# Windowed attention and a squared-ReLU block in one kernel: larger Q and K load chunks, immediate activation biases, and one deadline key for all engine orders

## The chip, the cores and the metric

The kernel runs on one core of a Trainium2 chip. The metric is the device time of one execution in microseconds (us), as a median of several executions. The profile is that of one execution; its span is about 1.8 us shorter than the time of that run. A run counts as slow when it took over 1.5% longer than the fastest run of the same kernel in its call; ratios are of fast runs alone.

Names of engines in the profile: PE is TensorE (matmuls), PEld its weight loads, DVE is VectorE, ACT is ScalarE, POOL is GpSimd and SPq the queue of SyncE. L467 is a line of the kernel's source.

## The reference

Attention with a window of 32 positions to each side, over 8 batches, 8 heads, 576 positions of 64 values. Its output, 4608 tokens of 512 values, goes through a feed-forward block of width 2048.

```python
scores = q @ k.T / sqrt(64);  mask = |i - j| <= 32        # per batch and head
attn   = softmax(where(mask, scores, -1e9)) @ v
x      = attn.transpose(0, 2, 1, 3).reshape(4608, 512)
h      = x @ w_in                                          # 512 -> 2048
out    = (s * relu(h)**2 + b) @ w_out                      # 2048 -> 512
```

All inputs are float32; the matmuls take bf16.

## The kernel before

The work is a graph of tasks. Each task has an engine, a modelled cost, the data that it reads and writes, and a key. A planner runs the graph once on modelled time, at every step taking the task that can start earliest, and among equals the one with the smallest key. The order so found becomes each engine's fixed instruction order, with the semaphore waits added. So the model of time decides the order, and on the chip an engine whose next instruction waits for a late load holds up everything behind it.

```python
c = (max(free[s], t.ready), t.key, t.n)         # the smallest c is placed next
...
if t.dma is not None:                           # a transfer: one modelled queue for all
    dma_free = max(dma_free, st + 1300.0) + t.dma[1]
    t.fin = dma_free + 700.0
```

One unit of attention is one batch, 192 positions (t = 0, 1, 2) and four heads (g2 = 0, 1): 48 units. Matmuls make the scores (sc), ScalarE the exponential (ex), VectorE multiplies by the mask, matmuls make row sums (ss) and values (av), ScalarE makes the reciprocal by Ln and Exp (rec), and VectorE writes the token columns (xt). The feed-forward block works on token blocks of 384, 128, 256, 384, then 512: for each block 16 groups of 4 matmuls (w), Relu (r), square (gt), then the second matmuls (o).

The q and k of batches 0 and 1 are loaded in three chunks of 192 rows on 96 partitions, cast by VectorE, transposed by TensorE and copied out of PSUM ("evacuated"). Unit 0 needs q chunk 0 and, for its window, k chunks 0 and 1; units 2 and 3 need k chunk 2 as well.

```python
def load2(b, n, t, waits=()):                               # 192 rows on 96 partitions
    ... STG[n][0:96, 2*t:2*t+2, :] ...  src[b, :, 192*t:192*t+192, :]
    key=key_of(b, -16), dma=("l", 768 * 27 / 16.0)

def key_of(b, part): return 16 * (b - 1) + part             # loads -16, casts -8, transposes -6
# attention unit number n: key = -100 + n      feed-forward: key = m + ft / 16

steps = [("q", 0), ("k", 0), ("k", 1), 0, ("q", 1), ("k", 2), 1, ("q", 2), 2]
e.activation(EX[e_][:, :, :], SC[:, :, :], AF.Exp, bias=ZERO_F[:, :], scale=0.125)
```

The softmax here doesn't subtract the row's maximum and nothing guards it: scores larger than these inputs give would overflow.

## Time and profile before

The median was 355.79 us (353.55 to 356.66, 4 runs).

To see where time is lost I count, for each stretch of time, the TensorE work done in it at full rate, from the weight loads in the trace. A w group is counted as its columns times 4 / 2.4 ns and an o matmul as 213 ns (in the trace, unhindered w matmuls of 384 columns start 0.163 us apart and o matmuls 0.215). Eight sc or ss matmuls are counted as 0.34 us, eight av as 0.22 and eight transposes as 0.43 (the trace has 0.33 for sc, 0.57 for ss and av together, and 0.44). This is an estimate. Elapsed time minus work is the "time lost" by TensorE.

| before, stretch of the span (us) | time lost | what the views show there |
|---|---|---|
| 0 to 42 | 30.0 | loads; the first w matmul starts at 35.4; all matmuls up to 40.0 run at half speed |
| 42 to 120 | 13.8 | waits of TensorE, and a spell of half clock |
| 120 to the end | 11.9 | no wait of note; 3.7 us of it after the last matmul |

The busy time of TensorE by stretch, before (stretch, its length, busy us and instructions, granted clock, DMA share, GB/s):

```profile
0.00:36.00 36.00, 14.90 (x187) 1.00 1.09 199
36.00:60.00 24.00, 23.82 (x158) 1.00 1.16 209
60.00:90.00 30.00, 26.64 (x303) 1.00 0.98 185
90.00:120.00 30.00, 24.82 (x227) 0.94 1.04 179
120.00:150.00 30.00, 29.58 (x256) 1.00 1.12 208
```

TensorE idles most before 36 us, then between 60 and 120 us. What it waited for, before (instruction and line, what released it: total us, times, longest):

```profile
PE w L431 <- DVE natq L414: 7.2, 2, 6.2
PE w L431 <- DVE natk L414: 6.8, 2, 5.5
PE ss L480 <- DVE ex L467: 5.6, 5, 2.2
PE o L577 <- DVE outs L589: 2.6, 1, 2.6
```

The first two are the head: transposes waiting for casts, which wait for loads. The last two are waits for VectorE in the middle. The timeline of VectorE in the head, before (start, us, instruction; in brackets the idle time ahead of it and what ended it):

```profile
12.21 1.01 DVE L436 COPY kt<-o 128x768 bf16<-128x768 bf16 x1
18.59 0.69 DVE L414 CAST natk<-stgk 96x1024 bf16<-96x1024 f32 x1 [5.37 <-DMA stgk<-in_k_dram]
19.20 0.42 DVE L390 CAST vb<-stgv 128x512 bf16<-128x512 f32 x1
20.20 1.01 DVE L436 COPY kt<-w 128x768 bf16<-128x768 bf16 x1 [0.58 <-PE w L431]
21.11 0.67 DVE L467 TENSOR_TENSOR ex<-ex,mask 128x1024 bf16<-128x1024 bf16 x1
```

VectorE stood for 5.4 us at the cast of a late k chunk; the mask of unit 0, ready since its exponential ended at 15.0 us, came after it at 21.1. The groups of ScalarE instructions, before (busy us, mean ns of one):

```profile
L464 ACT ACTIVATE ex<-sc,zero 128x1024 bf16<-128x1024 f32 x48 | 53.3, 1110 | 11.5 <-PE sc L457 11.4
L565 ACT ACTIVATE r_27<-w,zero 128x512 bf16<-128x512 f32 x24 | 16.5, 687 | 14.4 <-PE w L559 14.4
```

### The profile page before, as it was taken

The numbers are of one execution on the slowest core, as the hardware profiler recorded it, in microseconds if no ns is written. First come the engines' busy times: TensorE is split into PE (matmuls) and PEld (weight loads), VectorE is DVE, ScalarE is ACT, GpSimd is POOL, SyncE is SP. The second block draws the span as 40 slices with busy tenths as digits, with TensorE's granted clock in tenths as the row PEclk, the third lists the DMA queues.
The fourth block names the chain that finished last, engine by engine and source line by source line (L and its number), as shares of the span: only waits on it lengthen the run. The fifth ranks groups of instructions, "written<-read, shape, count | busy, mean of one in ns | idle before, by whom it ended". The sixth has DMA issues, their size and how long they took to land.

```text
span 353.1 us, 6377 instructions
## 1 busy us (share of the span) xinstructions
PE 316.8 (90%) x2502; PEld 161.2 (46%) x2544; DVE 208.9 (59%) x467; ACT 207.4 (59%) x324; POOL 49.4 (14%) x68
## 2 busy tenths in 40 slices
PE   1256999699976999999999999999999999999995
PEld 1134456465543444444444444444444444445542
DVE  4466368888696657866777767754345345432321
ACT  2249543678765668767777666666466456643310
POOL 8803023101530220130012000000000000000000
PEclk9999999999999899999999999999999999999999
DMA  7999999996998999999899997630000000010102
GB/s 167 211 210 207 221 203 200 207 219 122 189 216 160 196 188 200 210 223 174 187 196 183 173 218 174 127 105 32 30 32 30 32 30 32 30 61 30 59 38 83
DMA packets 107806, 49.45 MB, mean 140 GB/s; under 512 B 87552, under 2 KB 100864, under 8 KB 107776
## 3 DMA queue, kind: packets, MB, share of 16 engines
q1 hardware_dynamic: 100416, 35.40, 51.7%
q0 software_dynamic: 7360, 13.64, 19.9%
q8 instruction: 20, 0.33, 0.4%
q14 instruction: 10, 0.08, 0.1%
HBM read 36.70 MB, written 9.44 MB: 131 GB/s over the span
## 4 chain that ended last, share of the span: by engine, by line
PE 74%; DMA 12%; SPq 5%; DVE 4%; ACT 3%; issue 2%
PE o L577 32%; PE w L559 32%; DMA stgq<-in_q_dram 9%; PE ss L480 4%; SPq L309 4%; PE sc L457 3%; PE av L480 3%; DMA stgk<-in_k_dram 3%; SPq L320 1%; ACT ex L464 1%; DVE ex L467 1%; DVE vb L390 1%; DVE gt L568 1%; ACT rec L487 1%; DVE xt L494 1%
## 5 line engine op out<-in xcount | busy, mean ns | idle before, releaser
L559 PE MATMUL w<-xt,win 128*128 128x512 bf16 (+3 forms) x690 | 149.6, 346 | 2.6 <-ACT r_28 L565 0.9
L577 PE MATMUL o<-wout,gt 128*128 128x512 bf16 x548 | 140.0, 380 | 4.7 <-DVE outs L589 2.6
L559 PEld LDWEIGHTS w<-xt,win 128*128 128x128 bf16 x704 | 64.0, 99 | 66.2 <-issue 3.2
L577 PEld LDWEIGHTS o<-wout,gt 128*128 128x128 bf16 x576 | 53.2, 98 | 60.5 <-DVE outs L589 2.8
L464 ACT ACTIVATE ex<-sc,zero 128x1024 bf16<-128x1024 f32 x48 | 53.3, 1110 | 11.5 <-PE sc L457 11.4
L309 POOL DMA_DIRECT2D stgv<-in_v_dram x48 | 39.8, 833 | 139.6 <-DVE vb L390 104.3
L565 ACT ACTIVATE r_26<-w,zero 128x512 bf16<-128x512 f32 (+3 forms) x44 | 26.8, 608 | 28.9 <-PE w L559 28.2
L467 DVE TENSOR_TENSOR ex<-ex,mask 128x1024 bf16<-128x1024 bf16 x48 | 33.1, 689 | 17.8 <-ACT ex L464 17.1
L565 ACT ACTIVATE r_29<-w,zero 128x512 bf16<-128x512 f32 (+3 forms) x44 | 26.8, 608 | 21.5 <-PE w L559 21.1
L565 ACT ACTIVATE r_27<-w,zero 128x512 bf16<-128x512 f32 (+3 forms) x44 | 26.8, 609 | 21.0 <-PE w L559 20.5
L565 ACT ACTIVATE r_28<-w,zero 128x512 bf16<-128x512 f32 (+3 forms) x44 | 26.8, 608 | 20.2 <-PE w L559 20.2
L487 ACT ACTIVATE rec<-ss,zero 128x384 f32<-128x384 f32 x48 | 27.7, 576 | 17.2 <-PE ss L480 17.1
L589 DVE SCALAR_TENSOR_TENSOR outs<-o,sb_34,cvec 128x512 f32<-128x512 f32 x36 | 26.9, 748 | 13.7 <-PE o L577 13.7
L494 DVE TENSOR_TENSOR xt<-av,rec 128x384 bf16<-128x384 f32 x48 | 26.5, 553 | 8.6 <-ACT rec L490 4.5
L490 ACT ACTIVATE rec<-rec,zero 128x384 f32<-128x384 f32 x48 | 29.4, 612 | 0.7
L568 DVE TENSOR_TENSOR gt<-r_29 128x512 bf16<-128x512 bf16 (+3 forms) x44 | 16.4, 373 | 21.3 <-ACT r_29 L565 21.0
L568 DVE TENSOR_TENSOR gt<-r_28 128x512 bf16<-128x512 bf16 (+3 forms) x44 | 16.4, 373 | 20.3 <-ACT r_28 L565 20.2
L568 DVE TENSOR_TENSOR gt<-r_27 128x512 bf16<-128x512 bf16 (+3 forms) x44 | 16.4, 374 | 19.4 <-ACT r_27 L565 19.1
L480 PE MATMUL ss<-ex,ones 128*64 128x128 bf16 x384 | 21.2, 236 | 7.2 <-DVE ex L467 5.6
L568 DVE TENSOR_TENSOR gt<-r_26 128x512 bf16<-128x512 bf16 (+3 forms) x44 | 16.4, 373 | 13.9 <-ACT r_26 L565 13.8
L480 PEld LDWEIGHTS ss<-ex,ones 128*64 128x64 bf16 x384 | 13.0, 115 | 25.0 <-DVE ex L467 7.5
L390 DVE CAST vb<-stgv 128x512 bf16<-128x512 f32 (+1 forms) x48 | 21.0, 443 | 4.9 <-PE av L480 4.1
(52 smaller groups left out, 154.7 us busy)
## 6 DMA issues: line engine op xcount, KB each, us to landing
out_dram<-outs SPq DMA_DIRECT2D x36, 256.0 KB, 2.4
stgq<-in_q_dram SPq DMA_DIRECT2D x24, 256.0 KB, 5.5
stgk<-in_k_dram SPq DMA_DIRECT2D x24, 256.0 KB, 5.6
stgv<-in_v_dram POOLq DMA_DIRECT2D x16, 256.0 KB, 7.1
stgv<-in_v_dram POOLq DMA_DIRECT2D x16, 192.0 KB, 7.9
stgq<-in_q_dram SPq DMA_DIRECT2D x6, 384.0 KB, 13.4
stgk<-in_k_dram SPq DMA_DIRECT2D x6, 384.0 KB, 12.0
stgv<-in_v_dram POOLq DMA_DIRECT2D x16, 128.0 KB, 5.9
```

What stands on the lines that cost most here:

```text
L309: lambda e: e.dma_start(STG[n][p0:p1, blk, :].rearrange("p (h d) -> p h d", h=H), src_of[n][b, :, s0:s0 + ns, :].rearrange("h s d -> s h d ...
L464: add("act", lambda e: e.activation(EX[e_][:, :, :], SC[:, :, :], AF.Exp, bias=ZERO_F[:, :], scale=0.125), 1130.0, reads=[("SC", 0), ("SC" ...
L467: add("dve", lambda e: e.tensor_tensor(EX[e_][:, :, :], EX[e_][:, :, :], MASK[:, :, :], ALU.mult), 700.0, reads=[("E", e_), "MASK"], write ...
L480: fns.append(lambda e, u=u, a=a, hh=hh, dst=dst, lhs=lhs: e.matmul(dst[64 * hh:64 * hh + 64, 192 * u + 64 * a:192 * u + 64 * a + 128], lhs ...
L487: add("act", lambda e: e.activation(REC[e_][:, :], SS[:, 0:384], AF.Ln, bias=ZERO_F[:, :], scale=1.0), 600.0, reads=["SS", "ZERO"], writes ...
L490: add("act", lambda e: e.activation(REC[e_][:, :], REC[e_][:, :], AF.Exp, bias=ZERO_F[:, :], scale=-1.0), 600.0, reads=[("REC", e_), "ZERO ...
L494: add("dve", lambda e: e.tensor_tensor(XT[:, prs[0]:prs[1] + 1, x0:x0 + 192], AV[:, 0:384].rearrange("p (u c) -> p u c", u=2), REC[e_][:, ...
L559: add("pe", [lambda e, kc=kc: e.matmul(W[wb][:, 0:nt], lhsT=WIN_BF[:, kc, ft * 128:(ft + 1) * 128], rhs=XT[:, kc, t0:t0 + nt], start=(kc = ...
L565: add("act", lambda e: e.activation(R1[rb][:, 0:nt], W[wb][:, 0:nt], AF.Relu, bias=ZERO_F[:, :], scale=1.0), 280 + 0.82 * nt, reads=[("W", ...
L568: add("dve", lambda e: e.tensor_tensor(GT[gs][:, ft, 0:nt], R1[rb][:, 0:nt], R1[rb][:, 0:nt], ALU.mult), 160 + 0.53 * nt, reads=[("R1", rb ...
L577: add("pe", [lambda e, fc=fc: e.matmul(O[ob][:, :], lhsT=GT[gs][:, fc, sub * 128:sub * 128 + 128], rhs=WOUT_BF[:, fc, :], start=(fc == 0), ...
L589: add("dve", lambda e: e.scalar_tensor_tensor(OUTS[us][:, :], O[ob][:, :], SB128[:, 0:1], CVEC[:, :], ALU.mult, ALU.add), 760, reads=[("O" ...
```

## The change

It has three parts. Q and K of batches 0 and 1 come in chunks of 256 rows on 128 partitions (256, 256 and 64 rows), so unit 0 needs one chunk each of q and k; every chunk is evacuated in two halves. Activations take an immediate bias. Every key is on one scale, the feed-forward position at which the result is due, and the planner's transfers are modelled a little later. The diff, cut to its core:

```diff
+    DMALAT = 600.0
-                    r = t.fin + (100.0 if t.dma is not None else t.lat)
+                    r = t.fin + (self.DMALAT if t.dma is not None else t.lat)
...
         def key_of(b, part):
-            return 16 * (b - 1) + part
+            if b == 0:
+                return -100 + part
+            t = min(2, max(0, int(part + 0.5)))
+            return rel[b, t, 0] / 16.0 + 0.1 * (part - t) - (0 if part >= 0 else 0.5)
...
-        def load2(b, n, t, waits=()):                      # 96 partitions, 192 rows
+        CHUNKS = [(256 * c, min(128, (S - 256 * c) // 2)) for c in range((S + 255) // 256)]
+        def load2(b, n, c, waits=()):
+            s0, ns = CHUNKS[c]
...          # transpose_pe: two halves r = 0, 1; batch 0: r = 0 on ScalarE, r = 1 on VectorE
-            add(evac, fn, 900, reads=[res], writes=grans(n, slot, 192 * t, 192 * t + 192), key=key)
+                add(evac, fn, 200 + 4 * ns / 1.0, reads=[res],
+                    writes=grans(n, slot, s0, s0 + 2 * ns), key=key, accum=(r == 1))
...          # keys: first two v blocks of batch 0 -2000; casts, copies and units by key_of
-            key = -100 + n
+            key = key_of(b, t + 0.1 * g2)
...
-                steps = [("q", 0), ("k", 0), ("k", 1), 0, ("q", 1), ("k", 2), 1, ("q", 2), 2]
+                steps = [("q", 0), ("k", 0), 0, ("k", 1), ("q", 1), 1, ("k", 2), ("q", 2), 2]
...
-            ... AF.Exp, bias=ZERO_F[:, :], scale=0.125)    # and Ln, Exp, Relu
+            ... AF.Exp, bias=0.0, scale=0.125)
```

More of the change, by code (lines that the diff above doesn't have):

```diff
@@ L259, in bass_sliding_window_symmetric__then__act_starrelu_kernel @@
         IDENT = sb((128, 128), BF16, "ident")
-        ZERO_F = sb((128, 1), F32, "zero")
         GT = [sb((128, 16, 512), BF16, "gt") for _ in range(2)]
@@ L286, in bass_sliding_window_symmetric__then__act_starrelu_kernel, with first_block @@
         NPE = 2
-        EVAC0 = {"q": "act", "k": "dve"}
+        EVACS = [("act", "dve"), ("dve", "dve")]
+        def first_block(tok):
+            return next(m for m in range(NM) if TBLK[m][0] + TBLK[m][1] > tok)
+        rel, nxt = {}, 1e9
+        for b in range(B - 1, 0, -1):
+            for t in range(NT3 - 1, -1, -1):
+                for g2 in (1, 0):
+                    nxt = min(nxt - PACE, 16 * first_block(b * S + 192 * t) - LEAD)
+                    rel[b, t, g2] = nxt
         src_of = {"q": q, "k": k, "v": v}
@@ L312, in load @@
                 ),
-                900.0 if n == "v" else 1070.0, writes=[("STG", n, blk)], key=key_of(b, -16), waits=waits,
-                dma=("v" if n == "v" else "l", ns * 9.3))
-        def load2(b, n, t, waits=()):
+                900.0 if n == "v" else 1070.0, writes=[("STG", n, blk)], waits=waits,
+                key=-2000 if b == 0 and n == "v" and blk < 2 else key_of(b, -5),
+                dma=("v" if n == "v" else "l", ns * 9.4))
+        CHUNKS = [(256 * c, min(128, (S - 256 * c) // 2)) for c in range((S + 255) // 256)]
+        def load2(b, n, c, waits=()):
+            s0, ns = CHUNKS[c]
             return add(
@@ L320, in load2 @@
                 lambda e: e.dma_start(
-                    STG[n][0:96, 2 * t:2 * t + 2, :].rearrange("p a (h x) -> p (a h) x", h=NPAIR),
-                    src_of[n][b, :, 192 * t:192 * t + 192, :].rearrange("h (p r) d -> p h (r d)", r=2),
-                ),
-                1000.0, writes=[("STG", n, 2 * t), ("STG", n, 2 * t + 1)], key=key_of(b, -16), waits=waits,
-                dma=("l", 768 * 27 / 16.0))
+                    STG[n][0:ns, 2 * c:2 * c + 2, :].rearrange("p a (h x) -> p (a h) x", h=NPAIR),
+                    src_of[n][b, :, s0:s0 + 2 * ns, :].rearrange("h (p r) d -> p h (r d)", r=2),
+                ),
+                1000.0, writes=[("STG", n, 2 * c), ("STG", n, 2 * c + 1)], key=key_of(b, -5), waits=waits,
+                dma=("l", 8 * ns * 26 / 16.0))
         def load_weights(which, i, waits=()):
@@ L335, in load_weights @@
                     moe_w_out.rearrange("(fc p) c -> p fc c", p=128)[:, 4 * i:4 * i + 4, :])
-            return add("pool", fn, 1000.0, writes=[("W" + which, i)], waits=waits, key=-30,
+            return add("pool", fn, 1000.0, writes=[("W" + which, i)], waits=waits, key=key_of(0, 0),
                        dma=("w", 2550.0))
-        for n, t in (("q", 0), ("k", 0), ("k", 1), ("q", 1), ("k", 2), ("q", 2)):
-            load2(0, n, t)
+        for n, c in (("q", 0), ("k", 0), ("k", 1), ("q", 1), ("k", 2), ("q", 2)):
+            load2(0, n, c)
         for blk in range(6):
             load(0, "v", blk)
-        add("dve", lambda e: e.memset(ZERO_F[:], 0.0), 100, writes=["ZERO"], key=-99)
-        add("dve", lambda e: e.memset(ONESW[:], 1.0), 150, writes=["ONESW"], key=-99)
-        add("dve", lambda e: e.memset(ONES[:], 1.0), 150, writes=["ONES"], key=-99)
-        add("dve", lambda e: e.memset(ONES[0:WIN, 1, :], 0.0), 100, writes=["ONES"], key=-98)
-        add("dve", lambda e: e.memset(ONES[128 - WIN:128, 2, :], 0.0), 100, writes=["ONES"], key=-98)
+        add("dve", lambda e: e.memset(ONESW[:], 1.0), 150, writes=["ONESW"], key=-2001)
+        add("dve", lambda e: e.memset(ONES[:], 1.0), 150, writes=["ONES"], key=-2001)
+        add("dve", lambda e: e.memset(ONES[0:WIN, 1, :], 0.0), 100, writes=["ONES"], key=-2000)
+        add("dve", lambda e: e.memset(ONES[128 - WIN:128, 2, :], 0.0), 100, writes=["ONES"], key=-2000)
         for slot in range(2):
@@ L352, in bass_sliding_window_symmetric__then__act_starrelu_kernel @@
                 add("dve", lambda e, slot=slot, c0=c0: e.memset(KT[slot][:, :, c0:c0 + WIN], 0.0), 150,
-                    writes=[("KTPAD", slot)], key=-98)
+                    writes=[("KTPAD", slot)], key=-2000)
         for (p0, blk) in ((0, 0), (128 - WIN, 2 * NT3 - 1)):
             add("dve", lambda e, p0=p0, blk=blk: e.memset(STG["v"][p0:p0 + WIN, blk, :], 0.0), 350,
-                writes=[("STGPAD", blk)], key=-98)
+                writes=[("STGPAD", blk)], key=-2000)
         add("pool", [lambda e: e.dma_start(SB128[:, 0:1], moe_s.partition_broadcast(128)),
                      lambda e: e.dma_start(SB128[:, 1:2], moe_b.partition_broadcast(128))],
-            2000.0, writes=["SB128"], dma=("w", 200.0), key=-60)
+            2000.0, writes=["SB128"], dma=("w", 200.0), key=key_of(0, 4))
         def band(tile, res, lo, hi):
@@ L366, in band @@
                                           channel_multiplier=-1),
-                350, reads=["ONESW"], writes=[res], key=-70)
+                350, reads=["ONESW"], writes=[res], key=-1900)
             add("pool",
@@ L371, in band @@
                                           channel_multiplier=1),
-                350, reads=[res], writes=[res], key=-70)
+                350, reads=[res], writes=[res], key=-1900)
         band(IDENT[:, :], "IDENT", 0, 0)
@@ L377, in bass_sliding_window_symmetric__then__act_starrelu_kernel @@
         add("dve", lambda e: e.tensor_copy(MASK[:, 0, 256:512], MASK[:, 0, 0:256]), 200,
-            reads=["MASK"], writes=["MASK"], key=-40)
+            reads=["MASK"], writes=["MASK"], key=key_of(0, -0.3))
         add("dve", lambda e: e.tensor_copy(MASK[:, 1, :], MASK[:, 0, :]), 250,
-            reads=["MASK"], writes=["MASK"], key=-40)
+            reads=["MASK"], writes=["MASK"], key=key_of(0, -0.3))
         wts = [load_weights("in" if i < 4 else "out", i % 4) for i in range(8)]
@@ L386, in cast_v @@
             slot = b % 2
-            key = key_of(b, -8)
+            key = key_of(b, blk // 2 - 0.3)
             pad = [("STGPAD", blk)] if blk in (0, 2 * NT3 - 1) else []
@@ L402, in cast @@
             add("dve", lambda e: e.tensor_copy(NAT[n][0:ns, blk, :], STG[n][0:ns, blk, :]),
-                400.0, reads=[("STG", n, blk)], writes=[("NAT", n, blk)], key=key_of(b, -8))
+                400.0, reads=[("STG", n, blk)], writes=[("NAT", n, blk)], key=key_of(b, max(0, 128 * blk - WIN) // 192 - 0.5))
         def transpose_dma(b, n, blk):
@@ L410, in transpose_dma, with cast2 @@
                 1250.0, reads=[("NAT", n, blk)], writes=grans(n, slot, s0, s0 + ns),
-                dma=("t", 1000.0), key=key_of(b, -6))
-        def cast2(b, n, t):
+                dma=("t", 1000.0), key=key_of(b, max(0, 128 * blk - WIN) // 192 - 0.4))
+        def cast2(b, n, c):
+            ns = CHUNKS[c][1]
             add("dve", lambda e: e.tensor_copy(
-                NAT[n][0:96, 2 * t:2 * t + 2, :].rearrange("p r (h d) -> p r h d", h=H),
-                STG[n][0:96, 2 * t:2 * t + 2, :].rearrange("p a (g r d) -> p r (a g) d", r=2, d=D)),
-                700.0, reads=[("STG", n, 2 * t), ("STG", n, 2 * t + 1)],
-                writes=[("NAT", n, 2 * t), ("NAT", n, 2 * t + 1)], key=key_of(b, -8))
+                NAT[n][0:ns, 2 * c:2 * c + 2, :].rearrange("p r (h d) -> p r h d", h=H),
+                STG[n][0:ns, 2 * c:2 * c + 2, :].rearrange("p a (g r d) -> p r (a g) d", r=2, d=D)),
+                700.0, reads=[("STG", n, 2 * c), ("STG", n, 2 * c + 1)],
+                writes=[("NAT", n, 2 * c), ("NAT", n, 2 * c + 1)], key=key_of(b, c - 0.5))
@@ L420, in bass_sliding_window_symmetric__then__act_starrelu_kernel, with transpose_pe @@
         tcount = {"n": 0}
-        def transpose_pe(b, n, t, banks, evac):
+        def transpose_pe(b, n, c, banks, evacs):
             slot = b % 2
+            s0, ns = CHUNKS[c]
             dst = QT[slot] if n == "q" else KT[slot]
-            res, bank = banks[tcount["n"] % len(banks)]
-            tcount["n"] += 1
-            view = bank.bitcast(BF16)[:, 0:768].rearrange("p (r g c) -> p r g c", r=2, g=NPAIR)
-            c0 = 192 * t + (0 if n == "q" else WIN)
-            to = dst[:, :, c0:c0 + 192].rearrange("p g (x r) -> p r g x", r=2)
-            key = key_of(b, -6)
-            add("pe", [lambda e, r=r, pr=pr: e.transpose(view[:, r, pr, :],
-                                                         NAT[n][0:96, 2 * t + r, pr * 128:(pr + 1) * 128],
-                                                         IDENT[0:96, 0:96])
-                       for r in range(2) for pr in range(NPAIR)],
-                450, reads=[("NAT", n, 2 * t), ("NAT", n, 2 * t + 1), "IDENT"], writes=[res], key=key)
-            fn = (lambda e: e.copy(to, view)) if evac == "act" else (lambda e: e.tensor_copy(to, view))
-            add(evac, fn, 900, reads=[res], writes=grans(n, slot, 192 * t, 192 * t + 192), key=key)
@@ new lines, in transpose_pe @@
+            c0 = s0 + (0 if n == "q" else WIN)
+            key = key_of(b, c - 0.4)
+            for r in range(2):
+                res, bank = banks[tcount["n"] % len(banks)]
+                tcount["n"] += 1
+                view = bank.bitcast(BF16)[:, 0:512].rearrange("p (g c) -> p g c", g=NPAIR)[:, :, 0:ns]
+                to = dst[:, :, c0:c0 + 2 * ns].rearrange("p g (x r) -> p r g x", r=2)[:, r]
+                add("pe", [lambda e, pr=pr, r=r, view=view: e.transpose(
+                    view[:, pr, :], NAT[n][0:ns, 2 * c + r, pr * 128:(pr + 1) * 128], IDENT[0:ns, 0:ns])
+                    for pr in range(NPAIR)],
+                    270, reads=[("NAT", n, 2 * c), ("NAT", n, 2 * c + 1), "IDENT"], writes=[res], key=key)
+                evac = evacs[r]
+                fn = ((lambda e, to=to, view=view: e.copy(to, view)) if evac == "act" else
+                      (lambda e, to=to, view=view: e.tensor_copy(to, view)))
+                add(evac, fn, 200 + 4 * ns / 1.0, reads=[res],
+                    writes=grans(n, slot, s0, s0 + 2 * ns), key=key, accum=(r == 1))
@@ L461, in unit @@
                             start=True, stop=True))
-            add("pe", fns, 310.0, reads=qk_res, writes=[("SC", 0), ("SC", 1)], key=key + (0.5 if b > 0 else 0),
+            add("pe", fns, 310.0, reads=qk_res, writes=[("SC", 0), ("SC", 1)], key=key + (0.05 if b > 0 else 0),
                 after=after + ([("av", n - 1)] if b > 0 else []), name=("qk", n))
             add("act", lambda e: e.activation(EX[e_][:, :, :], SC[:, :, :], AF.Exp,
-                                              bias=ZERO_F[:, :], scale=0.125),
-                1130.0, reads=[("SC", 0), ("SC", 1), "ZERO"], writes=[("E", e_)], key=key)
+                                              bias=0.0, scale=0.125),
+                1040.0, reads=[("SC", 0), ("SC", 1)], writes=[("E", e_)], key=key)
             add("dve", lambda e: e.tensor_tensor(EX[e_][:, :, :], EX[e_][:, :, :], MASK[:, :, :],
@@ L487, in unit @@
             add("act", lambda e: e.activation(REC[e_][:, :], SS[:, 0:384], AF.Ln,
-                                              bias=ZERO_F[:, :], scale=1.0),
-                600.0, reads=["SS", "ZERO"], writes=[("REC", e_)], key=key)
+                                              bias=0.0, scale=1.0),
+                500.0, reads=["SS"], writes=[("REC", e_)], key=key)
             add("act", lambda e: e.activation(REC[e_][:, :], REC[e_][:, :], AF.Exp,
-                                              bias=ZERO_F[:, :], scale=-1.0),
-                600.0, reads=[("REC", e_), "ZERO"], writes=[("REC", e_)], key=key)
+                                              bias=0.0, scale=-1.0),
+                500.0, reads=[("REC", e_)], writes=[("REC", e_)], key=key)
             x0 = b * S + q0
@@ L498, in unit @@
                 560.0, reads=["AV", ("REC", e_)], writes=[("XT", b, t, g2)], key=key)
-        def first_block(tok):
-            return next(m for m in range(NM) if TBLK[m][0] + TBLK[m][1] > tok)
-        rel, nxt = {}, 1e9
-        for b in range(B - 1, 0, -1):
-            for t in range(NT3 - 1, -1, -1):
-                for g2 in (1, 0):
-                    nxt = min(nxt - PACE, 16 * first_block(b * S + 192 * t) - LEAD)
-                    rel[b, t, g2] = nxt
         for b in range(B):
@@ L535, in bass_sliding_window_symmetric__then__act_starrelu_kernel @@
                     cast2(b, *x)
-                    transpose_pe(b, *x, banks, EVAC0[x[0]] if b == 0 else "dve")
+                    transpose_pe(b, *x, banks, EVACS[b])
                     continue
@@ L565, in s1 @@
             add("act", lambda e: e.activation(R1[rb][:, 0:nt], W[wb][:, 0:nt], AF.Relu,
-                                              bias=ZERO_F[:, :], scale=1.0),
-                280 + 0.82 * nt, reads=[("W", wb), "ZERO"], writes=[("R1", rb)], key=key)
+                                              bias=0.0, scale=1.0),
+                190 + 0.82 * nt, reads=[("W", wb)], writes=[("R1", rb)], key=key)
             add("dve", lambda e: e.tensor_tensor(GT[gs][:, ft, 0:nt], R1[rb][:, 0:nt], R1[rb][:, 0:nt],
```

## The prediction

> **What bounds the kernel now.** Three parts, from the timeline and the busy time by stretch.
> (1) Head, 0 to 35.4 us: the first w<-xt,win matmul starts at 35.4, after only some 13 us of TensorE work. Loads bound it: the DMA share is above 1.1 from 8 us on. The traced packets show how: the SyncE queue (q, k; 512-byte packets, about 45 ns) has moved 1.8 MB by 12 us but needs until 24 us for the last 0.5 MB, because the GpSimd queue (v, weights; about 3 KB and 230 ns a packet) takes the engines. The Trainium skill ("DMA: Bandwidth & Descriptors", on arbitration) says an engine alternates between queues packet by packet; this agrees. Engine order adds to it: the exp of unit 0 ends at 15.0 us, its mask multiply starts at 21.1, since VectorE, in order, first sits 5.4 us on the third k chunk (landed at 18.6).
> (2) 35.4 to 120 us: about 69 us of matmul work (estimate from matmul counts at 2.4 columns/ns) takes 84.6. The TensorE waits show 2.6 us at 64.6 (VectorE held by batch 1's last q chunk), 1.8 at 99.5, 0.9 at 111, 2.2 at 114 (VectorE holding casts of late loads): planning errors rather than bandwidth, the DMA share being 0.95 at 80 to 120. A half-clock spell near 115 us costs 1.7.
> (3) After 120 us TensorE never waits: 230 us, and 3.7 of tail.
>
> **What the change does.**
> - 256-row chunks: unit 0 needs one q and one k chunk (1.05 MB) instead of three of 0.39 MB. The first two v blocks move ahead, so k lands no earlier than about 9 us. The middle units need the first 512 rows of q and k (2.1 MB), on the traced curve there at 18 to 20 us. The last q/k landing of batch 0 stays near 24 us: same bytes.
> - Evacuation: 6 copies of 1.01 us become 12 smaller ones split between ScalarE and VectorE: about -0.3 us latency per chunk.
> - Immediate bias: the Trainium skill ("ScalarE: Activation LUTs", What ACT_TABLE_LOAD costs) gives 280 ns + 0.833 N with a pointer, 186 + 0.833 N without. The trace has 1110 ns for N=1024, 687 for 512; I expect 1020 and 595. Some 320 x 93 ns = 30 us of ScalarE (59% busy), hidden after 120 us; in the head 0.25 us per unit, and block 0's 16 W groups, paced by two banks and ScalarE, gain about 0.7. In all 1 us.
> - New keys and later landings in the plan: the 6 us VectorE block in the head should go; attention of batches 1 to 3 should be placed where its data has come, saving 3 to 5 us of waits between 60 and 120.
>
> **Sum.** First w matmul at about 30 us (-5.5), ScalarE -1, middle waits -4: 355.8 - 10 = about 346.
>
> **Right or wrong.** Right: mask multiply of unit 0 before 15 us; first w matmul at 28 to 32; TensorE waits after it under 4 us; ex activation 1.02 us; part (3) still about 230 us. Wrong if: VectorE again waits on a late chunk ahead of ready work; weights issued sooner starve the second q and k chunks beyond 22 us; or TensorE, now earlier, waits near 60 us for batch 1.
>
> Predicted 346.0 us, 8 in 10 between 339.5 and 352.5; faster by over 2%: 0.67, within 2%: 0.29, slower: 0.04.

## The result, and the profile after

The kernel after took 345.86 us in the median (345.07 to 346.57, 4 runs). The ratio is 0.973, with a 95% interval of 0.968 to 0.978. (A ratio is the mean time of one kernel's fast runs over that of the other's of the same rounds, so it is not quite the ratio of the medians.)

TensorE by stretch, after:

```profile
0.00:36.00 36.00, 18.02 (x206) 1.00 1.11 211
36.00:60.00 24.00, 23.79 (x182) 1.00 1.14 220
60.00:90.00 30.00, 29.16 (x310) 1.00 0.95 199
90.00:120.00 30.00, 25.93 (x247) 1.00 1.11 190
120.00:150.00 30.00, 29.58 (x243) 1.00 1.12 202
```

Busy time in the stretch from 60 to 90 us rose from 26.6 to 29.2 us. In time lost (elapsed minus work at full rate; the repeat is the unchanged kernel after in a later call):

| stretch (us) | before | after | gain | repeat |
|---|---|---|---|---|
| 0 to 42 | 30.0 | 25.7 | 4.3 | 25.1 |
| 42 to 60 | 0.1 | 0.4 | -0.3 | 0.3 |
| 60 to 90 | 5.6 | 2.6 | 3.0 | 2.6 |
| 90 to 120 | 8.1 | 5.6 | 2.5 | 2.4 |
| 120 to the end | 11.9 | 13.0 | -1.1 | 13.2 |

The span fell by 8.3 us (353.1 to 344.8), 4.3 of them in the head, although the first w matmul moved by 5.4 (35.4 to 30.0). Part of what had stood before that matmul, attention of the last two units of batch 0, now stands behind it: the scores of one unit and the row sums and values of two, less one group of values that was behind it before, 1.2 us of work (an estimate from the same counts). A marker that moves by 5.4 us is not a gain of 5.4 us. Nor does the place of the cut leave the gain alone: cut at 36 us, in the middle of the half speed of before, the head would seem to gain only 2.1 us.

What TensorE waited for, after:

```profile
PE w L452 <- DVE natq L433: 9.5, 1, 9.5
PE o L452 <- DVE natq L433: 4.4, 1, 4.4
PE sc L480 <- DMA kt<-natk: 3.4, 1, 3.4
PE ss L503 <- DVE ex L490: 1.5, 5, 0.4
```

Waits for VectorE in the middle are down to 0.4 us each. One wait of 3.4 us is new, for a transposing transfer of k. VectorE in the head, after:

```profile
13.96 0.73 DVE L458 COPY kt<-o 128x512 bf16<-128x512 bf16 x1 [0.67 <-ACT kt L457]
18.97 0.69 DVE L433 CAST natq<-stgq 128x1024 bf16<-128x1024 f32 x1 [4.28 <-DMA stgq<-in_q_dram]
19.58 0.72 DVE L458 COPY kt<-w 128x512 bf16<-128x512 bf16 x1
20.31 0.42 DVE L408 CAST vb<-stgv 64x512 bf16<-64x512 f32 x1
20.77 0.69 DVE L490 TENSOR_TENSOR ex<-ex,mask 128x1024 bf16<-128x1024 bf16 x1
```

The block is still there: the mask of unit 0 starts at 20.8 us, behind 4.3 us of waiting for the second q chunk. The plan thought that chunk would land at 10.8 us.

Score matmuls of units 0 to 3 start at 13.3, 20.1, 22.8 and 25.9 us before, and at 14.7, 20.7, 22.5 and 25.1 after: hardly different. But the columns of unit 3, which the first w matmul needs, are written at 34.5 us before and at 29.9 after. The difference arises after the scores. ScalarE before, in that stretch (cut):

```profile
28.27 1.13 ACT L464 ACTIVATE ex<-sc,zero 128x1024 bf16<-128x1024 f32 x1
30.41 1.11 ACT L464 ACTIVATE ex<-sc,zero 128x1024 bf16<-128x1024 f32 x1 [0.51 <-PE sc L457]
31.42 0.57 ACT L487 ACTIVATE rec<-ss,zero 128x384 f32<-128x384 f32 x1
32.23 1.11 ACT L464 ACTIVATE ex<-sc,zero 128x1024 bf16<-128x1024 f32 x1 [0.24 <-PE sc L457]
33.24 0.60 ACT L490 ACTIVATE rec<-rec,zero 128x384 f32<-128x384 f32 x1
```

And after (cut):

```profile
25.74 1.02 ACT L487 ACTIVATE ex<-sc 128x1024 bf16<-128x1024 f32 x1 [0.59 <-PE sc L480]
28.22 0.49 ACT L510 ACTIVATE rec<-ss 128x384 f32<-128x384 f32 x1 [0.30 <-PE ss L503]
28.74 0.52 ACT L513 ACTIVATE rec<-rec 128x384 f32<-128x384 f32 x1
29.59 1.02 ACT L487 ACTIVATE ex<-sc 128x1024 bf16<-128x1024 f32 x1 [0.33 <-PE sc L480]
```

Some 2.5 of the 4.6 us are there at the start of unit 3's exponential (28.3 us against 25.7): before, ScalarE first did the copy of the third q chunk (26.4 us), the reciprocal of unit 1 and half of that of unit 2. The rest comes next: before, the exponentials of units 4 and 5 (30.4 and 32.2 us) ran ahead of the end of unit 3's reciprocal, 33.8. After, that reciprocal ends at 29.3 and the exponential of unit 4 follows it. The same ScalarE groups after:

```profile
L487 ACT ACTIVATE ex<-sc 128x1024 bf16<-128x1024 f32 x48 | 49.1, 1022 | 10.5 <-PE sc L480 9.6
L578 ACT ACTIVATE r_27<-w 128x512 bf16<-128x512 f32 x24 | 14.3, 597 | 16.5 <-PE w L572 15.2 <-DVE outs L602 1.1
```

An activation is 88 to 90 ns shorter.

### The profile page after: what moved, and what is told of

Its sections match the earlier page's. It is cut to its first block, busy times and chain, and to the rows that moved or that the text cites. A ratio compares the mean times of both kernels' runs of the same rounds, so it can differ in the third digit from the quotient of the medians.

```text
span 344.8 us, 6390 instructions
## 1 busy us (share of the span) xinstructions
PE 314.9 (91%) x2504; PEld 159.8 (46%) x2544; DVE 211.2 (61%) x475; ACT 181.6 (53%) x327; POOL 48.1 (14%) x68
## 4 chain that ended last, share of the span: by engine, by line
PE 83%; DMA 7%; DVE 4%; issue 2%; SPq 1%; ACT 1%; DVEq 0%
PE w L572 36%; PE o L590 35%; DMA stgq<-in_q_dram 4%; PE ss L503 4%; PE sc L480 4%; PE av L503 3%; DMA kt<-natk 3%; PE o L611 1%; DVE vb L408 1%; DVE xt L517 1%; SPq L339 1%; ACT ex L487 1%; PE sc L452 1%; DVE ex L490 1%; DVE natk L420 0%
## 5 line engine op out<-in xcount | busy, mean ns | idle before, releaser
L572 PE MATMUL w<-xt,win 128*128 128x512 bf16 (+3 forms) x689 | 146.3, 342 | 2.3 <-issue 1.1
L572 PEld LDWEIGHTS w<-xt,win 128*128 128x128 bf16 x704 | 62.8, 98 | 61.1 <-DVE xt L517 0.9
L324 POOL DMA_DIRECT2D stgv<-in_v_dram x48 | 38.9, 812 | 140.5 <-DVE vb L408 121.0
L487 ACT ACTIVATE ex<-sc 128x1024 bf16<-128x1024 f32 x48 | 49.1, 1022 | 10.5 <-PE sc L480 9.6
L578 ACT ACTIVATE r_26<-w 128x512 bf16<-128x512 f32 (+3 forms) x44 | 22.9, 520 | 28.2 <-PE w L572 26.2
L578 ACT ACTIVATE r_25<-w 128x512 bf16<-128x512 f32 (+3 forms) x44 | 22.8, 518 | 26.2 <-PE w L572 24.0
L578 ACT ACTIVATE r_27<-w 128x512 bf16<-128x512 f32 (+3 forms) x44 | 22.8, 519 | 23.3 <-PE w L572 22.0
L578 ACT ACTIVATE r_28<-w 128x512 bf16<-128x512 f32 (+3 forms) x44 | 22.8, 519 | 23.1 <-PE w L572 23.0
L510 ACT ACTIVATE rec<-ss 128x384 f32<-128x384 f32 x48 | 23.4, 488 | 21.6 <-PE ss L503 21.5
L602 DVE SCALAR_TENSOR_TENSOR outs<-o,sb_33,cvec 128x512 f32<-128x512 f32 x36 | 26.9, 748 | 12.0 <-PE o L590 11.7
L517 DVE TENSOR_TENSOR xt<-av,rec 128x384 bf16<-128x384 f32 x48 | 26.6, 554 | 10.8 <-PE av L503 8.0
L581 DVE TENSOR_TENSOR gt<-r_26 128x512 bf16<-128x512 bf16 (+3 forms) x44 | 16.4, 374 | 21.5 <-ACT r_26 L578 21.3
L581 DVE TENSOR_TENSOR gt<-r_27 128x512 bf16<-128x512 bf16 (+3 forms) x44 | 16.4, 374 | 20.9 <-ACT r_27 L578 20.9
L581 DVE TENSOR_TENSOR gt<-r_28 128x512 bf16<-128x512 bf16 (+3 forms) x44 | 16.4, 373 | 18.4 <-ACT r_28 L578 18.1
L513 ACT ACTIVATE rec<-rec 128x384 f32<-128x384 f32 x48 | 24.9, 519 | 0.7
L480 PE MATMUL sc<-qt,kt 64*128 64x128 bf16 x384 | 20.3, 229 | 3.7 <-DMA kt<-natk 3.4
L503 PEld LDWEIGHTS ss<-ex,ones 128*64 128x64 bf16 x384 | 12.8, 114 | 20.2 <-issue 5.3
## 6 DMA issues: line engine op xcount, KB each, us to landing
stgk<-in_k_dram SPq DMA_DIRECT2D x4, 512.0 KB, 12.8
```

Of the source, the lines that this page charges most:

```text
L324: lambda e: e.dma_start(STG[n][p0:p1, blk, :].rearrange("p (h d) -> p h d", h=H), src_of[n][b, :, s0:s0 + ns, :].rearrange("h s d -> s h d ...
L480: fns.append(lambda e, u=u, pr=pr, a=a, hh=hh: e.matmul(SC[:, hh, 256 * u + 128 * a:256 * u + 128 * a + 128], lhsT=KT[slot][64 * hh:64 * h ...
L487: add("act", lambda e: e.activation(EX[e_][:, :, :], SC[:, :, :], AF.Exp, bias=0.0, scale=0.125), 1040.0, reads=[("SC", 0), ("SC", 1)], wr ...
L503: fns.append(lambda e, u=u, a=a, hh=hh, dst=dst, lhs=lhs: e.matmul(dst[64 * hh:64 * hh + 64, 192 * u + 64 * a:192 * u + 64 * a + 128], lhs ...
L513: add("act", lambda e: e.activation(REC[e_][:, :], REC[e_][:, :], AF.Exp, bias=0.0, scale=-1.0), 500.0, reads=[("REC", e_)], writes=[("REC ...
L517: add("dve", lambda e: e.tensor_tensor(XT[:, prs[0]:prs[1] + 1, x0:x0 + 192], AV[:, 0:384].rearrange("p (u c) -> p u c", u=2), REC[e_][:, ...
```

## The experiments

Twelve kernels ran, in four calls; all gave right results. The kernel before ran in each call too, with medians of 356.8, 356.5, 357.1 and 355.5 us. The last column is time lost in the profiled run. Every profiled run was fast.

| run | what it is | median us (range) | first w matmul | lost to 42 / 42 to 120 / rest |
|---|---|---|---|---|
| before | | 355.79 (353.55 to 356.66) | 35.4 | 30.0 / 13.8 / 11.9 |
| after | | 345.86 (345.07 to 346.57) | 30.0 | 25.7 / 8.6 / 13.0 |
| a_again | after, unchanged | 344.39 (342.84 to 348.87) | 29.5 | 25.1 / 5.3 / 13.2 |
| b_imm | before, immediate biases | 355.03 (352.66 to 357.37) | 37.0 | 31.0 / 15.3 / 11.8 |
| a_ptr | after, pointer biases | 344.70 (343.70 to 345.49) | 30.3 | 27.4 / 5.6 / 13.1 |
| a_192 | after, old chunks | 349.51 (348.09 to 350.09) | 32.7 | 27.4 / 6.0 / 15.4 |
| a_oldkeys | after, old keys and transfer model | 351.72 (351.11 to 353.30) | 35.1 | 28.7 / 9.4 / 14.4 |
| a_oldmodel | after, old transfer model | 348.20 (344.64 to 348.49) | 28.9 | 25.1 / 9.6 / 14.5 |
| a_late | after, head's true landings, third chunks kept back | 353.81 (352.20 to 355.98) | 28.2 | 27.6 / 10.9 / 17.2 |
| a_late8 | a_late, later loads 8 us later in the plan | 349.30 (346.66 to 352.35) | 28.3 | 25.7 / 12.9 / 12.8 |
| a_holdk | a_late's idea, weights issued later | 350.19 (346.94 to 351.36) | 27.0 | 24.3 / 14.5 / 13.3 |
| a_hold8 | a_holdk, later loads 8 us later in the plan | 348.85 (345.86 to 351.53) | 28.5 | 25.3 / 7.7 / 17.3 |
| a_par | after, halves evacuated without waiting for each other | 348.35 (346.30 to 351.01) | 29.1 | 25.1 / 5.1 / 17.9 |
| a_swap | after, one move in the head | 344.85 (342.70 to 347.84) | 28.5 | 24.3 / 6.5 / 14.3 |

Medians and ranges hold every run. One run each of a_again, a_late8, a_hold8 and a_swap was slow; their fast runs alone have medians of 342.9, 348.0, 348.2 and 344.4. Of a_late's 27.6, 2.6 us are one wait at 39.4 us. The expectation of the repeat, which is the yardstick of its call:

> The kernel after once more, unchanged, as the yardstick of this call: 345 to 346 us, first w matmul at 30 us, and qk of unit 2 at 22.5 us.

Two fast runs of one kernel differ by up to 5 us in the last three calls. The two profiles of the kernel after show one reason: the 3.4 us wait for the transposing transfer is in one and absent from the other. Differences under 2 us between runs of different calls say nothing here.

### The biases

Theory: ScalarE's shorter instructions give about 1 us (the prediction's term). Rival: ScalarE paces the head, so they give 3.

```diff
-  e.activation(EX[e_][:, :, :], SC[:, :, :], AF.Exp, bias=ZERO_F[:, :], scale=0.125)
+  e.activation(EX[e_][:, :, :], SC[:, :, :], AF.Exp, bias=0.0, scale=0.125)     # b_imm; a_ptr is the reverse
```

No engine's order changes in either, apart from the one memset of the bias tile that a_ptr needs.

> The kernel before with immediate biases alone; every engine's order is unchanged. Arithmetic theory (the prediction's ScalarE term): 1 us off, about 354.8 us, first w matmul near 34.5 us. Rival theory (ScalarE paces the head, since it is 6.6 us busy in the 8 us from 24 to 32): 3 us or more off, first w matmul before 33 us.

> The kernel after with the biases as [128,1] pointers again; every engine's order is unchanged. Prediction's ScalarE term: about 1 us slower than the kernel after (347 us), ex activation back to 1.11 us. Rival (ScalarE paces the head): 2.5 us or more slower (348.5 or more).

Measured: b_imm took 355.03 us beside 356.8, but its ratio is 1.001 (0.991 to 1.011), and its first w matmul came at 37.0, not by 34.5. a_ptr took 344.70 us beside 356.8, ratio 0.971 (0.964 to 0.978), the same as the kernel after within error, with its ex back at the old length. So no gain is seen from the 26 us of ScalarE time that the change saves (207.4 to 181.6 us busy), and a_ptr shows no sign of the rival's 2.5 us. The intervals are 2.5 to 3.5 us wide to each side, so the 1 us of the prediction is not excluded.

### The chunks, and the keys

Theory (the prediction): the chunks bring the head's gain. Rival: engine order does, since the scores start at the same times in both kernels.

```diff
 # a_192: load2, cast2, transpose_pe and the step order of before; keys on the new scale by the unit that needs the chunk
-        CHUNKS = [(256 * c, ...)]
+        load2: 192 rows on 96 partitions, one evacuation copy a chunk
 # a_oldkeys: every key, DMALAT and the transfer costs of before; 256-row chunks kept
-            t = min(2, max(0, int(part + 0.5)))
-            return rel[b, t, 0] / 16.0 + ...
+            return 16 * (b - 1) + part
```

> The kernel after with the 192-row chunks, single evacuation copies and step order of before, new keys and immediate biases kept. Prediction (the head's 5.4 us come from the chunks' data arrival): first w matmul back at 34 us or later, 350 us or more. Rival (the head's gain is order and ScalarE time, since the qk matmuls of units 2 and 3 start at 22.8 and 25.9 us before and 22.5 and 25.1 after): first w matmul at 31 us or earlier, at most 347.5 us.

> The kernel after with the keys and the transfer model of before; 256-row chunks and immediate biases kept. Prediction: the head keeps its gain (first w matmul by 31 us), the middle waits come back (about 8 us in all after 36 us), about 350 us. Rival (order makes the head's gain): first w matmul at 33 us or later, 352 us or more.

Measured: without the chunks 349.51 us, first w at 32.7, ratio 0.985 (0.979 to 0.991). Without the keys 351.72 us, first w at 35.1, ratio 0.993 (0.987 to 0.998). Both miss the stated numbers of one side or the other: a_192 lies between the two theories, a_oldkeys fits the rival in its head and nearly in its time. Both parts are needed for the whole gain, the keys for somewhat more of it. Taking the kernel after at 342.9 to 345.9 (fast runs), the old chunks cost 4 to 7 us and the old keys 6 to 9. Up to 42 us, where the kernel after lost 25.7 and 25.1 us, a_192 lost 27.4 and a_oldkeys 28.7: of the head's gain, some 2 us hang on the chunks and some 3 on the keys. In the middle the keys' share is not clear: a_oldkeys lost 9.4 us between 42 and 120, against 8.6 and 5.3 in the kernel after and 13.8 before, so part of that gain came without the new keys.

How the old keys act on the new chunks is seen in a_oldkeys, where the second q chunk landed at 18.1 us, as early as elsewhere. VectorE then did this (its timeline, cut):

```profile
18.12 0.69 DVE L428 CAST natq<-stgq 128x1024 bf16<-128x1024 f32 x1 [6.47 <-DMA stgq<-in_q_dram]
...
26.54 0.43 DVE L403 CAST vb<-stgv 128x512 bf16<-128x512 f32 x1
26.88 0.72 DVE L453 COPY qt<-o 128x512 bf16<-128x512 bf16 x1
```

The evacuation of that chunk's second half waited until 26.9 us, behind eight casts of v, two masks, two token blocks and two casts of third chunks. Unit 2's scores started at 27.7 us instead of 22.5. In the kernel after the same copy runs at 21.4 us, with one cast of v between the landing and it; the other casts of v and those of the third chunks follow it. VectorE is busy from the landing on, so what it does first is what counts. In the kernel before, with the same keys and the old chunks, unit 2's scores started in time (22.8 us), and the delay came on ScalarE, as shown above.

### The transfer model alone

```diff
-    DMALAT = 600.0
+    DMALAT = 100.0
-  dma=... ns * 9.4      / 8 * ns * 26 / 16.0
+  dma=... ns * 9.3      / 8 * ns * 27 / 16.0
```

> The kernel after with the transfer model of before (latency 100 ns, old cost of a descriptor), its keys kept. If the keys alone make the gain of the middle: within 1.5 us of the kernel after, 344 to 347 us. If the transfer model does: waits after 36 us grow by 3 us or more, 348 us or more.

Measured: 348.20 us (344.64 to 348.49), ratio 0.975 (0.967 to 0.983). The median is at the edge of the second expectation, the ratio is that of the kernel after, and its profile has the same large wait as the kernel after (2.8 us, for the transposing transfer; a second, of 1.5 us, ends at 170.8). So it stays open whether the model is worth 0 or 3 us. Built but not run: with the latency alone put back, one instruction of the whole program changes its place.

### The block of VectorE in the head

Theory (the prediction): VectorE standing at a late chunk ahead of a ready mask costs several us. Rival: units 2 and 3 need that chunk anyway. a_swap moves only the cast of that chunk and what hangs on it behind the masks of units 0 and 1, in the finished order (the edit in words):

```diff
+        lo = index of the cast of q chunk 1;  hi = index of the mask of unit 1
+        late = {cast} and every task between lo and hi that depends on it
+        order = order[:lo] + (tasks not in late) + (tasks in late) + order[hi + 1:]
```

> The kernel after with one move in the finished order: the cast of the second q chunk of batch 0 and what hangs on it (4.3 us of VectorE waiting for a load) stand behind the masks of units 0 and 1; every later instruction keeps its place on its engine. Prediction (the block is worth several us): first w matmul at 27 us or earlier and 342 us or less. Rival (units 2 and 3 need that chunk, landed near 18.7 us, so at most the work of units 0 and 1 that now lies behind it comes off): masks of unit 0 at 12 us, first w matmul at 27.5 to 29 us, and what is gained there only partly kept, 343 to 345.5 us.

VectorE in a_swap:

```profile
16.45 0.69 DVE L499 TENSOR_TENSOR ex<-ex,mask 128x1024 bf16<-128x1024 bf16 x1 [0.48 <-ACT ex L496]
18.17 0.69 DVE L499 TENSOR_TENSOR ex<-ex,mask 128x1024 bf16<-128x1024 bf16 x1 [0.58 <-ACT ex L496]
18.78 0.69 DVE L441 CAST natq<-stgq 128x1024 bf16<-128x1024 f32 x1
```

The mask of unit 0 now starts at 16.5 us, not at the 12 us expected, since its exponential ends only then; 4.3 us of standing are gone. The first w matmul came at 28.5 us, 1.0 to 1.4 earlier than in the two profiles of the kernel after, and 24.3 us were lost up to 42 us, against 25.7 and 25.1. The time is 344.85 us (ratio 0.971, 0.965 to 0.977), not distinguishable from the kernel after. This fits the rival: the block was worth about 1 us, and what is left of the head's delay agrees with the landing of the second q chunk as its gate.

### Telling the plan the truth, and letting the queue go first

These runs correct the landings that the plan assumes, and then move the weights' transfers.

```diff
 # a_late: planned landings of batch 0 as measured, third chunks kept back (27.3 and 28.9 us; they land at 20.4 and 22.2)
+  extra = {("q", 1): 8200, ("k", 1): 2600, ("k", 2): 15500, ("q", 2): 15500}     # ns, plan only
 # a_holdk: the same idea, and
-  load_weights(which, i)
+  load_weights(which, i, waits=[load of k chunk 1])
+  load(1, "v", blk, waits=[a load of w_in])
 # a_late8, a_hold8: planned landings of batch 1 and later 8 us later as well
```

> The kernel after, but the plan is told when the head's loads landed in the trace (second q chunk 19 us instead of the 10.8 it assumes) and keeps the third chunks back, so VectorE does the masks of units 0 and 1 before it waits for that chunk. Prediction (the VectorE block ahead of the mask is worth several us): first w matmul at 26 to 27 us, about 342.5 us. Rival (the block is covered by the wait for the second q chunk, which gates units 2 and 3 whatever the order): first w matmul at 28.5 to 30 us, 344.5 to 346 us.

> The same, and the weights' transfers are issued only when the second k chunk of batch 0 has landed (near 10.5 us instead of 7.8). If the GpSimd queue's large packets starve the q chunk: it lands near 15 us instead of 19, first w matmul at 25.5 to 27 us, 341 to 343 us. If bytes alone decide: q still lands at 18 us or later and the time is that of the run without the hold.

> The run with the third chunks kept back (353.8 us, 9 us worse than the kernel after although its first w matmul came 1.3 us earlier), with one more change to the plan alone: loads of batch 1 and later are assumed to land 8 us later, as they do on the chip (second q chunk of batch 1: plan 47.6 us, chip 59.4). Theory of cancelling errors (the plan of the kernel after puts TensorE 7.4 us too early and the loads 5 to 12 us too early, so that matmuls still meet their data; correcting only the head broke that): TensorE waits after 36 us fall from 9 us to under 3, 342 to 346 us. Rival (holding the third chunks back is itself what costs): 350 us or more.

> Weights issued after the second k chunk landed, with the same 8 us on later loads in the plan. Cancelling errors: the head's gain of the hold (first w matmul at 27.0 us against 29.5) is now kept, 341 to 344 us. Rival: later loads arrive too late for a TensorE that starts earlier, waits near 60 and 100 us stay, 347 us or more.

Measured: a_late starts its first w at 28.2 us and takes 353.81 us, 8 to 11 us more than the kernel after, which neither theory had. Its waits of TensorE between 36 and 130 us:

```profile
PE ss L503 <- DVE ex L490: 6.1, 4, 4.0
PE av L503 <- DVE xt L517: 2.6, 1, 2.6
```

In a_holdk the q chunk landed at 16.7 us, against 18.5 in the unchanged kernel of the same call, and the first w matmul came at 27.0. That is half of what "starved by large packets" asked for. The head was, with a_swap's, the best of all, 24.3 us lost up to 42, yet the time was 350.19 us, with waits of 2.0 and 4.4 us in the middle.

The plan explains part of this. It has the first w matmul of the kernel after at 22.6 us, 7.4 too early, and the loads of batch 1 at 42.6 to 48.4 us, 4.6 to 12 too early. Matmuls and loads are wrong by similar amounts, so their relative order is nearly right. a_late changes only the head and takes that agreement away. But it does not only put the head right: it plans the third chunks some 7 us later than they land. With the later loads shifted too, a_late8 gained 4.5 us on a_late (348.0 in its fast runs), but its remaining waits are not under 3 us, as expected of the theory:

```profile
PE sc L480 <- DMA kt<-natk: 3.5, 1, 3.5
PE ss L503 <- DVE ex L490: 2.3, 2, 1.8
```

a_hold8 came to 348.85 us, also short of its 341 to 344. So "errors that cancel" is supported by the recovery of a_late8, not settled: the time of a_late8 (349.3, fast runs 348.0) lies between its own 342 to 346 and the 350 of the rival, that keeping the third chunks back is what costs, and each change of the model also reshuffles several hundred instructions. The longest wait left in a_late8 is for a transposing transfer of k. In the kernel after that one transfer took 8.7 us from issue to landing. Why it was so long stays open.

### Halves that wait for each other

In the kernel after ScalarE's half of an evacuation ends at 10.88 us and VectorE's starts at 10.91: the graph makes the second writer wait for the first. a_par gives each half its own name.

```diff
-  writes=grans(n, slot, s0, s0 + 2 * ns), key=key, accum=(r == 1)
+  writes=[x for x in grans(n, slot, s0, s0 + 2 * ns) if x[3] == r], key=key
```

> The kernel after, but the second half of a chunk's evacuation no longer waits for the first (in the trace of after ScalarE's half ends at 10.88 us and VectorE's starts at 10.91, though the prediction had them side by side). If that wait costs: 0.7 us per chunk on the way to unit 0 and to units 2 and 3, first w matmul 0.5 to 1.5 us earlier, 344 to 345 us. If VectorE is busy with other work anyway: no difference beyond 0.5 us.

Measured: 348.35 us. The halves do overlap (they start at 9.92 and 10.44 us), and the first w matmul came at 29.1 us, 0.4 earlier than in the repeat, with the same 25.1 us lost up to 42. After 120 us it lost 17.9 us against 13.2. Well over a third of its instructions' places had changed, so the run doesn't say what the wait itself costs; it says only that the head gains at most half a microsecond from it.

No run beats the kernel after beyond its spread.

## Why the prediction was right or wrong

The time was right: 346.0 predicted, 345.86 measured. The sum behind it was not: its terms were off by 1 us and more, in both directions.

- **First w matmul at 30 us: right** (29.96). But the prediction booked all of the 5.4 us as gain. The time lost up to 42 us fell by 4.3 us (4.9 in the repeat), since 1.2 us of attention work moved behind the marker. The failed step is "First w matmul at about 30 us (-5.5)" as a term of the sum.
- **Its cause: partly wrong.** The step "The middle units need the first 512 rows of q and k (2.1 MB), on the traced curve there at 18 to 20 us" was right as a number (18.95; "k lands no earlier than about 9 us" was not, the first k chunk landed at 7.2), but before, the third k chunk had landed at 18.6, and units 2 and 3 started their scores at the same times in both kernels. A larger part of the gain lies in what VectorE and ScalarE do after that landing (a_oldkeys, some 3 us). a_192 shows that the chunks have a share, some 2 us of time lost and 2.7 us of the marker.
- **"The 6 us VectorE block in the head should go": wrong.** It stayed, at 4.3 us, because the plan still has the chunk 8.2 us too early; the mask of unit 0 started at 20.8 us, not before 15. And it hardly mattered: without it (a_swap) the head is about 1 us shorter and the time the same.
- **"Split between ScalarE and VectorE: about -0.3 us latency per chunk": wrong.** The halves ran one after the other, 1.49 us from the start of the first to the end of the second (10.15 to 11.64) against one copy of 1.01.
- **Immediate bias: sizes right** (1022 and 597 ns, against 1020 and 595), **worth not seen**: "In all 1 us" does not show in b_imm and a_ptr, which could not have told 1 us from nothing.
- **"Saving 3 to 5 us of waits between 60 and 120": too small.** Time lost fell by 5.5 us there in the profile of after and by 8.7 in its repeat (13.7 to 5.0). The waits themselves, under 4 us predicted, are 4.3 us in the three of 0.4 us or more of the first profile and 0.9 in the repeat. That the new keys made this gain is not shown (a_oldkeys keeps part of it). The half-clock spell of before was put down as a loss and not followed up; its 1.7 us are in this sum.
- **Nothing gained after 120 us: right**; 1.1 us more was lost there. (As a length, "part (3) still about 230 us" did not hold: the last matmul ends 221 us after 120, since whatever was gained earlier leaves less work behind 120 us.)

So the term for the head was too large by about 1 us, that for ScalarE is not seen, 1 us was lost after 120 us, and between 42 and 120 us 5.2 us were gained (8.5 in the repeat) instead of 4. That the time was met within 0.2 us is in part luck: the two profiles of the kernel after alone differ by 3.7 us (344.8 and 341.1).

## What to carry to other kernels

Book a gain at the engine that ends last, as elapsed time minus work done, stretch by stretch; the moment at which some first instruction starts can move further than what is won (5.4 us against 4.3 here), because other work slides behind it. Put no cut inside a spell of half speed: here that would have halved the gain of the head. In a kernel whose orders come from a plan, ask what each in-order engine does first once the late load has landed, and put a deadline there. And be wary of correcting a plan's model in one place: changing the head alone cost 8 to 11 us here, of which about half came back when the later loads were shifted too (the cause is not settled). Every edit to a plan should be compared with a repeat of the unedited kernel; here small differences stay open.

## What the Trainium skill lacked or had wrong

- "TensorE: Matmul & The Clock Gate", Part 1, says that the array falls to half clock after at least one idle window of about 3.4 us, that the window runs freely, and that activity of that length releases it. The half-clock spells here do come in lengths of 3.4 and 6.8 us, and of the eleven that all profiles show before the last matmul, ten follow or overlap a wait of TensorE of 1.8 to 6.6 us (the eleventh follows two waits of 1.4 and 1.2 us). So waits shorter than a window sufficed: in the kernel before, a spell began at 115.1 us after a wait from 111.8 to 114.0. And longer ones did not always do it: a wait of 3.4 us in the kernel after (96.8 to 100.1) brought none; the w matmuls after it start 0.16 us apart, at full rate. A wait in the middle can so cost 1.7 us more than it shows. The kernel before, around that spell (columns as in the stretches above):

```profile
111.80:115.10 3.30, 1.09 (x20) 1.00 0.71 141
115.10:118.50 3.40, 3.40 (x18) 0.50 0.72 87
118.50:122.00 3.50, 3.45 (x31) 1.00 1.09 298
```

- The page on trace reading ("Perfetto Trace Analysis") has nothing on the granted clock; the clock-gate page warns that these records can be unreliable. A case of it: the clock column says 1.00 for the head, but four w matmuls of 384 columns take 1.46 us up to 33.3 us in the kernel after and 0.82 from 34.0 on. In the kernel before eight of them take 2.74 us at 35.4, and half speed ends at 40.0. The difference, 0.64 us, is the 4 x 384 / 2.4 ns that half speed would add (first line before, the others after):

```profile
35.37 2.74 PE L559 MATMUL w<-xt,win 128*128 128x384 bf16 x8
29.96 1.46 PE L572 MATMUL w<-xt,win 128*128 128x384 bf16 x4 [0.41 <-DVE xt L517]
31.89 1.46 PE L572 MATMUL w<-xt,win 128*128 128x384 bf16 x4
33.98 0.82 PE L572 MATMUL w<-xt,win 128*128 128x384 bf16 x4
```

- "ScalarE: Activation LUTs", What ACT_TABLE_LOAD costs, gives 93 ns for each pointer operand. The trace agrees (88 to 93 ns on four shapes). What no page could say is the worth in this kernel: no gain is seen, within 2.5 to 3.5 us.
- "DMA: Bandwidth & Descriptors", Queues, rings and completion order (on arbitration), has engines alternate between queues packet by packet, a packet being several descriptors. No run here tests it: holding back the queue with the large packets for 4.2 us let the other queue's chunk land at 16.7 instead of 18.5 us, as it would under any rule by which the two share the engines. In the kernel before the trace counts 399 packets started on the SyncE queue against 217 on the GpSimd queue between 12 and 16 us, and 226 against 742 between 20 and 24.
